# One input block moved between two filter loads, a re-rated planner, rotating PSUM slots, later reloads of q, longer bursts of zero matmuls

## The chip, the cores and the metric

The kernel runs on one core of one Trainium2 chip. The metric is device time in microseconds (us): the kernel before takes 185.58 us, the median of 13 runs that lie between 184.31 and 188.64. Engines are named as in the profile: PE is TensorE (PEld its weight loads), DVE is VectorE, ACT is ScalarE, POOL is GpSimd, SP is SyncE, which here only issues DMAs.

## What is computed

Two branches over the same 2048 x 640 input q are mixed by a gate. Cut to what matters:

```python
# branch A: shift, gate, long convolution by FFT over 2*S points
k_shift = sum(k_pad[:, t:t+S] * shift_k[:, ks-1-t] for t in range(4))
kv = k_shift * v
y  = irfft(rfft(pad(kv)) * rfft(pad(ssm_k)))[:S]   # along the sequence, per channel
a  = q * (y + kv * ssm_D)
# branch B: a token-mixing MLP
h = layernorm(q);  u = gelu(einsum("bsd,sf->bdf", h, w1) + b1)
b = (einsum("bdf,fs->bds", u, w2) + b2).transpose(0, 2, 1)
g = sigmoid((q * gate_w).sum(-1, keepdims=True))
out = g * a + (1 - g) * b                          # 2048 x 640, bf16
```

S is 2048, D (channels) 640, F (hidden tokens) 1536.

## The kernel before, in words

**Work.** The FFT is written as matmuls with a table of sines, `FTB`, followed by adds and subtractions on DVE. In order:

- The filter `ssm_k` is loaded (tile `ssm`), transposed on PE by blocks of 128 channels (`transp`, line 838), evicted from PSUM by ACT into `wT`, and transformed (`fwd` and `fwd_even`, lines 854 and 870) into the spectra `C`, first for half h=0, then for h=1. Each transform group is two or four matmuls of 320 columns and one eviction by ACT ("C<-pp").
- Meanwhile DVE computes the sine arguments (`pint`, line 801 on), which ACT turns into `FTB` (four sines, in the order p = 0, 2, 1, 3), and the layer norm of q: statistics of 16 row tiles ("stats<-X", `ln_tile`, line 913), a reciprocal root on POOL ("rstd"), and the scaling in place ("X<-X,mv,rstd", `ln_apply`, line 932).
- k is loaded (`kn`), permuted by DVE ("kp<-kn", `k_turn`, line 746), transposed by DMA (`KT`), convolved with the four taps on PE ("pp<-KF,KT"), multiplied by v on DVE, and transformed as the filter was.
- The MLP's first layer, 12 output tiles of 32 matmuls each ("pp<-X,ring", called m1 below, line 1057 on), fills PE wherever the above has nothing for it; after it the second layer ("pp<-GT,W", m2, line 1099 on) does so.
- DVE multiplies the spectra (`product`, `cross`, lines 1138 and 1178). Some of the sums are done by accumulating DMAs that POOL issues ("C<-SS", "C<-C"). `invmix` (line 1190) and `inverse` (line 1209) turn the products back; the result is multiplied by q, which is loaded a second time into `q_hi` (rows 0 to 1023) and `q_lo` (the rest), since X has been overwritten by the layer norm. `q_hi` first serves as scratch for the products.

**What orders the work.** No engine chooses at run time. Every operation is entered with an estimated duration and a priority into `_Sched` (line 324), and `run` (line 384) plays the list through: at each moment, each free engine takes the ready operation of lowest priority number. The order found is then emitted, per engine, as the program; each engine (and SP's DMA queue) goes through it strictly in order and waits on semaphores where data are missing. Matmuls of the convolution have their program index as priority, m1 10^6 and more, m2 2x10^6 and more, so the MLP fills gaps. For a DMA the planner takes bytes over a rate (`dma`, line 702: 365 GB/s unless told otherwise), one after another on a single `dma_free` clock, plus 2 us until the data count as landed, and 6 us more for DMAs of POOL (lines 455 to 460). Loads marked `chain=True` keep their program order among one another.

**PSUM.** There are four slots of two banks, `NSLOT = 4`. At most two are held by the MLP and three by the convolution (`limit`, line 333). A slot counts as free when the planner's clock has passed the end of its eviction; the free list is sorted before each take, so the lowest-numbered free slot is used (lines 450 to 453).

**The start.** SP issues `ssm` blocks (0,1), (1,3), (3,5) of half 0 (128, 256 and 256 channels; 256, 512 and 512 KB), then the four blocks of q into `X` (640 KB each), two rows of biases, half 1 of `ssm`, w1, k and so on (lines 765 to 778). Matmuls of zeros (`spin`, line 784) go ahead of each transposition of half 0: (6, 1, 1, 1, 1) of them for the five channel blocks. They have no data to wait for but the zero tile and the PSUM slot.

**The reloads.** The two loads of `q_hi` (line 1261) are entered after the first two products, so each goes out as soon as SP's queue reaches it and its half of the scratch has been read.

Of the kernel before, what the change touches and what calls it, by code (L numbers as in the profile page):

```python
# [18 lines left out]
class _Tracker:  # L19
# [230 lines left out]
        self.dma_sems[name] = sem  # L250
        self.dma_cnt[name] = 0

    def dma(self, stream, out_ap, in_ap, semname, transpose=False, noncontig=False, accum=False):
        reads = [in_ap] + ([out_ap] if accum else [])
        writes = [out_ap]
        acc = self.pre(stream, reads, writes)
        engobj = self.eng[stream]
        sem = self.dma_sems[semname]
        if transpose:
            ins = engobj.dma_start_transpose(out_ap, in_ap)  # L260
        elif accum:
            ins = engobj.dma_start(out_ap, in_ap, accum_op=ALU.add, max_dma_last_dim=2560)  # L262
        elif noncontig:
            with self.nc.allow_non_contiguous_dma(reason="tiny"):
                ins = engobj.dma_start(out_ap, in_ap)
        else:
            ins = engobj.dma_start(out_ap, in_ap)
        ins.then_inc(sem, 16)
        self.dma_cnt[semname] += 16
        v = self.dma_cnt[semname]  # L270
        self.dma_hist[(semname, v)] = dict(self.known[stream])
        src = ("dma", semname, v)
        for reg, mode in acc:
            self.add_record(reg, mode, src)
        return v
# [48 lines left out]
class _Sched:  # L324
# [59 lines left out]
    def run(self):  # L384
# [21 lines left out]
        nfree = list(range(self.NSLOT))  # L406
# [8 lines left out]
        while started < n:  # L415
            while frees and frees[0][0] <= t:
                _, sl, cls = heapq.heappop(frees)
                nfree.append(sl)
                held[cls] -= 1
            nxt = []  # L420
            progress = False
            for e in engs:
                while pend[e] and pend[e][0][0] <= t:
                    _, p, i = heapq.heappop(pend[e])
                    heapq.heappush(ready[e], (p, i))
                if free[e] > t:
                    nxt.append(free[e])
                    continue
                skipped = []
                pick = None  # L430
                while ready[e]:
                    p, i = heapq.heappop(ready[e])
                    op = ops[i]
                    if op.vt is not None and op.vt.slot is None:
                        c = op.vt.cls
                        if not nfree or held.get(c, 0) >= self.limit.get(c, 99):
                            skipped.append((p, i))
                            continue
                    pick = op
                    break  # L440
                for s in skipped:
                    heapq.heappush(ready[e], s)
                if pick is None:
                    if pend[e]:
                        nxt.append(pend[e][0][0])
                    continue
                op = pick
                progress = True
                started += 1
                if op.vt is not None and op.vt.slot is None:  # L450
                    nfree.sort()
                    op.vt.slot = nfree.pop(0)
                    held[op.vt.cls] = held.get(op.vt.cls, 0) + 1
                op.start = t
                if e in ("SP", "QA") or op.lat < 0:
                    issue = 1.2 if e == "POOL" else 0.1
                    s = max(t + issue, dma_free)
                    dma_free = s + op.dur
                    op.end = dma_free + 2.0 + (6.0 if e == "POOL" else 0.0)
                    free[e] = t + issue  # L460
                else:
                    op.end = t + op.dur
                    if op.lock:
                        op.end += max(port["POOL" if e == "DVE" else "DVE"] - t, 0.0)
                        port[e] = op.end
                    free[e] = op.end
                order.append(op)
                if op.vt is not None:
                    op.vt.left -= 1
                    if op.vt.left == 0:  # L470
                        heapq.heappush(frees, (op.end + 0.05, op.vt.slot, op.vt.cls))
                for s in op.asucc:
                    avail[s] = max(avail[s], op.start)
                    s.ndep -= 1
                    if s.ndep == 0:
                        heapq.heappush(pend[s.eng], (avail[s], s.prio, s.idx))
                for s in op.succ:
                    lat = 0.08 if s.eng == e else 0.15
                    if e == "PE" and s.eng == "PE":
                        lat = 0.0  # L480
                    avail[s] = max(avail[s], op.end + lat)
                    s.ndep -= 1
                    if s.ndep == 0:
                        heapq.heappush(pend[s.eng], (avail[s], s.prio, s.idx))
                nxt.append(free[e])
            if not progress:
                c = [x for x in nxt if x > t]
                if frees:
                    c.append(frees[0][0])
                assert c, "schedule stuck: " + str([(o.name, o.eng, o.ndep) for o in ops if not hasattr(o, "end")][:12])  # L490
                t = min(c)
# [19 lines left out]
def _build(nc, A_q, A_k, A_v, A_shift_k, A_ssm_k, A_ssm_D, B_x, B_w1, B_b1, B_w2, B_b2, gate_w, out):  # L511
    Bsz, S, D = A_q.shape
# [9 lines left out]
    with ExitStack() as es:  # L522
# [4 lines left out]
        for i in range(4):  # L527
            h = es.enter_context(nc.psum_tensor(f"pp{i}", [128, 1024], F32))
# [21 lines left out]
        def base_of(h):  # L550
            return T.mem[h.name][1]
# [26 lines left out]
        X = alloc("X", [128, 4, 4, D], BF16)  # L578
# [11 lines left out]
        ssm = alloc("ssm", [128, ND, S], BF16, at=base_of(C[3]))  # L590
# [14 lines left out]
        q_hi = alloc("q_hi", [128, 2, 4, D], BF16, at=base_of(Drow))  # L605
# [96 lines left out]
        def dma(o, i, nbytes, stream="SP", prio=None, sem=None, rate=365.0, chain=False, **kw):  # L702
            if sem is None:
                sem = f"d{ndma[0]}"
                ndma[0] += 1
            if sem not in T.dma_sems:
                T.add_dma_sem(sem, es.enter_context(nc.semaphore(f"s_{sem}")))
            rd = [i] + ([o] if kw.get("accum") else [])
            o_ = SC.add(stream, nbytes / rate / 1000.0, lambda s: T.dma({"QA": "ACT"}.get(stream, stream), o, i, sem, **kw), rd, [o], prio=prio, lat=-1.0, name="dma")
            if chain:  # L710
                if last[0] is not None:
                    o_.after.add(last[0])
                last[0] = o_
            return o_

        def dr(t, off, ap):
            return bass.AP(tensor=t.tensor, offset=t.offset + off, ap=ap)
# [8 lines left out]
            return lambda s: s[:, ci * 512:ci * 512 + 320]  # L726

        def ssm_load(h, a, b):
            dma(ssm[:, a:b, 1024 * h:1024 * h + 1024], dr(A_ssm_k, 128 * S * a + 1024 * h, [[S, 128], [128 * S, b - a], [1, 1024]]), 128 * (b - a) * 2048, chain=True)

        def row8(t, hk):
            return dr(t, (1024 * (hk // 2) + 4 * (hk % 2)) * D, [[8 * D, 128], [1, 4 * D]])
# [2 lines left out]
            return 16 + 128 * (1 - hk % 2)  # L735

        def x_load(hk):
            dma(X[:, hk, :, :], dr(A_q, 512 * hk * D, [[4 * D, 128], [1, 4 * D]]), 128 * 5120, chain=True)

        def w1_load(c, hk):  # L740
            dma(ring[c % 2][:, 4 * hk:4 * hk + 4, :], dr(B_w1, 512 * hk * F + 512 * c, [[4 * F, 128], [F, 4], [1, 512]]), 128 * 4096, chain=True)
# [23 lines left out]
        SSM0 = ((0, 1), (1, 3), (3, 5))  # L765
        SSM1 = ((0, 2), (2, 5))
        small(Drow[:, :], dr(A_ssm_D, 0, [[0, 1], [1, D]]), 1280, "QA")
        small(rows[0:20, 0, 0:128], dr(A_shift_k, 0, [[128, 20], [1, 128]]), 5120, "QA")
        for a, b in SSM0:
            ssm_load(0, a, b)  # L770
        for hk in range(4):
            x_load(hk)
        small(rows[0:4, 1, :], dr(B_b2, 0, [[512, 4], [1, 512]]), 4096, "SP", chain=True)
        small(rows[0:12, 2, 0:128], dr(B_b1, 0, [[128, 12], [1, 128]]), 3072, "SP", chain=True)
        for a, b in SSM1:
            ssm_load(1, a, b)
# [2 lines left out]

        zz = alloc("zz", [128, 512], BF16, at=base_of(GTB))  # L780
        memset("DVE", zz[:, :], 0.0, prio=-1)
        SPIN = (6, 1, 1, 1, 1)

        def spin(k):
            return [((lambda s: s[:, 0:512]), zz[:, 0:128], zz[:, :], True, True)] * k
# [271 lines left out]
        for ft in range(FT):  # L1057
# [20 lines left out]
            if ft in (1, 3, 5, 7):  # L1078
                hk = ft // 2
# [39 lines left out]
        A0 = {0: (C[2], 2), 1: (C[1], 0)}  # L1119
# [10 lines left out]
        def H(hs, c):  # L1130
            h, s = hs
            return V(h, s * SL + 1280 * c, [[SL, 2], [1, 1280]])
# [117 lines left out]
        def chained(f, *a):  # L1250
            n0 = len(SC.ops)
            f(*a)
            new = [o for o in SC.ops[n0:] if o.eng == "DVE"]
            for o in new:
                o.after.update(lastp[-1:])
            lastp.append(new[-1])
# [1 line left out]
        lastp = []  # L1258
        chained(product, A1[1], A1[1], V0[1], tmp_of(q_hi, 0), V1[1])
        chained(product, A1[0], A1[0], V0[0], tmp_of(q_hi, 1), V1[0])  # L1260
        for kt in range(2):
            dma(q_hi[:, kt, :, :], dr(A_q, 512 * kt * D, [[4 * D, 128], [1, 4 * D]]), 128 * 5120)
        acc_dma(A1[1], V1[1])
        acc_dma(A1[0], V1[0])
        chained(product, A0[1], A0[1], V0[1], H(V0[1], 0))
        chained(product, A0[0], A0[0], V0[0])
        for kt in range(2):
            dma(q_lo[:, kt, :, :], dr(A_q, (1024 + 512 * kt) * D, [[4 * D, 128], [1, 4 * D]]), 128 * 5120).after.add(w2last)
# [41 lines left out]
```

## Time and profile before

| what | value |
|---|---|
| median of 13 runs | 185.58 us (184.31 to 188.64) |
| the profiled execution | 184.66 us |
| its span, first to last instruction | 182.7 us |
| around the span (184.66 - 182.7) | 1.96 us |
| granted TensorE clock | 0.997 |
| PE busy / DVE busy / ACT busy / POOL busy | 172.5 / 171.6 / 117.4 / 39.1 us |
| DMA moved | 43.49 MB, mean 238 GB/s |

All moments below are microseconds from the start of the span. A line of the timeline gives start, duration, engine, source line, operation, output<-inputs, shape and count; in brackets stands how long the engine sat idle just before it, and which instruction ended that idle time. Most lines of the kernel record through helpers (L293 is every matmul, L669 every ACT operation, L625 every two-input DVE operation), so tiles tell operations apart, not lines. A busy PE is not PE at its peak: an interval of matmuls contains about 0.17 us of pipeline at its end.

### The profile page before, as it was taken

Reading aid. Unit: us, or ns where it says so; the run is one execution under the profiler, and the core shown is the slowest. Engines: PE = TensorE matmul, PEld = TensorE weight load, DVE = VectorE, ACT = ScalarE, POOL = GpSimd, SP = SyncE. Lnnn points to the kernel's source line nnn. Section 1 sums busy time; section 2 is a strip of 40 time slices with the busy share of each in tenths; the row PEclk is TensorE's granted clock in tenths of the full one; section 3 lists DMA queues with packets and bytes.
Section 4 is the critical chain, followed back from the end, with each engine's and each line's share of the span. In section 5 each row is a group of like instructions: output and inputs, shape, how many; then the busy total and the mean of one; then the engine's idle time right before and its main releaser. Section 6 shows DMA issues by size and latency. Waiting matters only on the chain.

```text
span 182.7 us, 3317 instructions
## 1 busy us (share of the span) xinstructions
PE 172.5 (94%) x1373; PEld 126.3 (69%) x1374; DVE 171.6 (94%) x203; ACT 117.4 (64%) x176; POOL 39.1 (21%) x42
## 2 busy tenths in 40 slices
PE   7878998979999999999999999999999999999991
PEld 2544584576778777776777778888888886778670
DVE  7799895999999999999998999999999979999975
ACT  5799988799989988149999931231312313761660
POOL 4059704000000055000510110403434000054000
PEclk9999999999999999999999999999999999999998
DMA  5999999999999989997499979699999998369584
GB/s 161 367 414 374 389 260 225 289 419 261 170 250 287 166 205 232 240 229 173 115 236 257 272 150 349 147 227 354 201 190 263 229 207 223 129 103 232 95 287 144
DMA packets 38541, 43.49 MB, mean 238 GB/s; under 512 B 15867, under 2 KB 31360, under 8 KB 38528
## 3 DMA queue, kind: packets, MB, share of 16 engines
q1 hardware_dynamic: 33296, 32.16, 59.3%
q0 software_dynamic: 5200, 11.14, 34.4%
q8 instruction: 10, 0.16, 0.4%
q14 instruction: 3, 0.02, 0.0%
q10 hardware_dynamic: 32, 0.01, 0.0%
HBM read 25.87 MB, written 2.62 MB: 156 GB/s over the span
## 4 chain that ended last, share of the span: by engine, by line
PE 38%; DVE 30%; ACT 18%; DMA 9%; issue 3%; DVEq 0%; SPq 0%
PE pp L293 38%; DVE C L625 21%; DMA C<-SS 7%; ACT C L669 5%; ACT gq L669 5%; DVE tm L625 4%; DMA ssm<-in_A_ssm_k_dram 3%; ACT FTB L669 2%; DVE q_hi L625 2%; ACT wT L669 2%; ACT GT L669 2%; DVE gq L625 1%; DVE SS L625 1%; ACT L669 1%; ACT ksh L669 1%
## 5 line engine op out<-in xcount | busy, mean ns | idle before, releaser
L625 DVE TENSOR_TENSOR C<-C 128x2560 bf16<-128x2560 bf16 (+2 forms) x37 | 54.7, 1522 | 1.3 <-DMA C<-SS 1.0
L293 PE MATMUL pp<-X,ring 128*128 128x320 bf16 x384 | 55.3, 299 | 0.0
L293 PE MATMUL pp<-GT,W 128*128 128x320 bf16 x384 | 52.8, 299 | 0.0
L293 PEld LDWEIGHTS pp<-GT,W 128*128 128x128 bf16 x384 | 43.5, 113 | 8.8 <-ACT cgb L669 0.2
L293 PEld LDWEIGHTS pp<-X,ring 128*128 128x128 bf16 x384 | 37.0, 98 | 15.2 <-DVE X L640 0.7
L669 ACT ACTIVATE C<-pp 128x640 bf16<-128x640 f32 x64 | 40.1, 726 | 5.4 <-PE pp L293 5.4
L669 ACT ACTIVATE O<-pp,c,omg 128x640 bf16<-128x640 f32 x15 | 13.3, 886 | 33.8 <-PE pp L293 33.8
L262 POOL DMA_DIRECT2D C<-C x8 | 10.9, 1609 | 46.5 <-DVE C L625 46.0
L293 PE MATMUL pp<-wT,FTB 128*128 128x320 bf16 x112 | 17.8, 300 | 1.6 <-ACT C L669 1.4
L669 ACT ACTIVATE cgb<-pp,gg 128x640 bf16<-128x640 f32 x16 | 12.7, 795 | 8.7 <-PE pp L293 8.7
L293 PEld LDWEIGHTS pp<-wT,FTB 128*128 128x128 bf16 x112 | 9.5, 98 | 8.8 <-ACT C L669 5.2
L919 DVE BATCH_NORM_STATS2 stats<-X 128x6 f32<-128x320 bf16 x32 | 13.7, 464 | 1.5 <-DMA X<-in_A_q_dram 1.5
L669 ACT ACTIVATE GT<-pp,cc 128x640 bf16<-128x640 f32 x12 | 9.4, 787 | 8.3 <-PE pp L293 8.2
L625 DVE TENSOR_TENSOR tm<-C,C 128x2560 bf16<-128x2560 bf16 (+1 forms) x7 | 14.3, 2057 | 0.0
L293 PE MATMUL pp<-C,FTB 128*128 128x320 bf16 x96 | 13.6, 299 | 0.2 <-DVE C L625 0.2
L262 POOL DMA_DIRECT2D C<-q_hi x6 | 5.9, 977 | 31.2 <-DVE C L625 16.2
L293 PEld LDWEIGHTS pp<-C,FTB 128*128 128x128 bf16 x96 | 9.0, 98 | 4.5 <-issue 0.5
L669 ACT ACTIVATE gq<-gq 128x640 bf16<-128x640 bf16 x16 | 11.6, 733 | 0.3 <-DVE gq L625 0.3
L625 DVE TENSOR_TENSOR SS<-C 128x2560 bf16<-128x2560 bf16 x8 | 11.7, 1486 | 0.1
L625 DVE TENSOR_TENSOR C<-tm 128x2560 bf16<-128x2560 bf16 (+1 forms) x9 | 10.6, 1192 | 0.1
L293 PE MATMUL pp<-KF,KT 128*128 128x128 bf16 (+1 forms) x160 | 9.0, 213 | 1.2 <-ACT GT L669 1.1
L669 ACT ACTIVATE wT<-pp 128x1024 bf16<-128x1024 f32 x10 | 9.5, 1034 | 0.8 <-PE pp L293 0.8
(73 smaller groups left out, 185.9 us busy)
## 6 DMA issues: line engine op xcount, KB each, us to landing
ring<-in_B_w_dram SPq DMA_DIRECT2D x12, 512.0 KB, 10.6
W<-in_B_w_dram SPq DMA_DIRECT2D x12, 512.0 KB, 7.3
C<-C POOLq DMA_DIRECT2D x8, 640.0 KB, 11.6
X<-in_A_q_dram SPq DMA_DIRECT2D x4, 640.0 KB, 8.8
kn<-in_A_k_dram SPq DMA_DIRECT2D x4, 640.0 KB, 9.5
out_dram<-O SPq DMA_DIRECT2D x7, 320.0 KB, 2.8
C<-SS POOLq DMA_DIRECT2D x3, 640.0 KB, 12.1
ssm<-in_A_ssm_k_dram SPq DMA_DIRECT2D x3, 512.0 KB, 6.1
```

Source lines behind the costliest of these rows:

```text
L262: ins = engobj.dma_start(out_ap, in_ap, accum_op=ALU.add, max_dma_last_dim=2560)
L293: ins = self.nc.tensor.matmul(ps_ap, lhsT=lhsT, rhs=rhs, start=start, stop=stop, skip_group_check=True)
L625: o_ = SC.add(eng, d, lambda s: T.op(eng, lambda e: e.tensor_tensor(o, a, b, op), rd, [o]), rd, [o], prio=prio, name="tt")
L669: return T.op("ACT", lambda e: e.activation(o, src, func, **kw), rr + [src], ww)
L919: ops.append(SC.add("DVE", 0.38, (lambda o, i: lambda s: T.op("DVE", lambda e: e.bn_stats(o, i), [i], [o]))(o, i), [i], [o]))
```

## The change

Five edits, in one diff:

- block 0 of q is loaded between the second and third filter loads of half 0;
- the planner's rates for some loads are set: 262 GB/s for the first `ssm` load, 195 for the two others of half 0, 385 for half 1, 410 for the blocks of q;
- the free list of PSUM slots is no longer sorted, so slots are taken in the order in which they came free;
- the bursts of zero matmuls are (7, 3, 3, 2, 2) long in place of (6, 1, 1, 1, 1);
- a DMA can be given tiles to wait for (`wait`, treated as extra reads), and the two loads of `q_hi` are entered after the third product and wait for `H(A0[1], 1)`, the half of a product which the accumulating DMA "C<-SS" completes. No arithmetic changes.


```diff
-    def dma(self, stream, out_ap, in_ap, semname, transpose=False, noncontig=False, accum=False):
-        reads = [in_ap] + ([out_ap] if accum else [])
+    def dma(self, stream, out_ap, in_ap, semname, transpose=False, noncontig=False, accum=False, wait=()):
+        reads = [in_ap] + ([out_ap] if accum else []) + list(wait)
...
                 if op.vt is not None and op.vt.slot is None:
-                    nfree.sort()
                     op.vt.slot = nfree.pop(0)
...
-            rd = [i] + ([o] if kw.get("accum") else [])
+            rd = [i] + ([o] if kw.get("accum") else []) + list(kw.get("wait", ()))
...
         def ssm_load(h, a, b):
-            dma(ssm[:, a:b, ...], dr(A_ssm_k, ...), 128 * (b - a) * 2048, chain=True)
+            dma(ssm[:, a:b, ...], dr(A_ssm_k, ...), 128 * (b - a) * 2048, chain=True, rate=(262.0 if a == 0 else 195.0) if h == 0 else 385.0)
...
         def x_load(hk):
-            dma(X[:, hk, :, :], dr(A_q, 512 * hk * D, ...), 128 * 5120, chain=True)
+            dma(X[:, hk, :, :], dr(A_q, 512 * hk * D, ...), 128 * 5120, chain=True, rate=410.0)
...
-        for a, b in SSM0:
+        for a, b in SSM0[:2]:
             ssm_load(0, a, b)
-        for hk in range(4):
+        x_load(0)
+        ssm_load(0, *SSM0[2])
+        for hk in range(1, 4):
             x_load(hk)
...
-        SPIN = (6, 1, 1, 1, 1)
+        SPIN = (7, 3, 3, 2, 2)
...
         chained(product, A1[0], A1[0], V0[0], tmp_of(q_hi, 1), V1[0])
-        for kt in range(2):
-            dma(q_hi[:, kt, :, :], dr(A_q, 512 * kt * D, [[4 * D, 128], [1, 4 * D]]), 128 * 5120)
         acc_dma(A1[1], V1[1])
         acc_dma(A1[0], V1[0])
         chained(product, A0[1], A0[1], V0[1], H(V0[1], 0))
+        for kt in range(2):
+            dma(q_hi[:, kt, :, :], dr(A_q, 512 * kt * D, [[4 * D, 128], [1, 4 * D]]), 128 * 5120, wait=[H(A0[1], 1)])
         chained(product, A0[0], A0[0], V0[0])
```

## Prediction

> **What bounds the kernel now.** I read the busy shares first, then busy time by stretch, then the timeline of the stretches that are not full, then the chain that ended last.
>
> ```profile
> PE 172.5 (94%) x1373; PEld 126.3 (69%) x1374; DVE 171.6 (94%) x203; ACT 117.4 (64%) x176; POOL 39.1 (21%) x42
> PEclk9999999999999999999999999999999999999998
> ```
>
> PE and DVE are equally full over the span. Where they are not full decides. Busy time by stretches of 4 us (PE, PEld, DVE, ACT, POOL, with instruction counts):
>
> ```profile
> 24.00:28.00 4.00, 4.00 (x50) 3.46 (x49) 4.00 (x11) 3.78 (x5) 0.00 (x0) 1.00 1.12 207
> 28.00:32.00 4.00, 3.12 (x21) 1.57 (x19) 1.85 (x8) 3.12 (x5) 2.11 (x3) 1.00 1.19 244
> 36.00:40.00 4.00, 2.77 (x51) 2.35 (x48) 4.00 (x4) 3.99 (x6) 0.00 (x0) 1.00 1.01 415
> 40.00:44.00 4.00, 4.00 (x46) 3.12 (x46) 3.94 (x5) 3.73 (x6) 0.00 (x0) 1.00 0.85 344
> ```
>
> From 40 to 176 PE shows 4.00 in every stretch but one (3.79 in 152:156). So PE's work from there is one block that ends when it ends: only what frees PE before 40 us can move the end, and DVE must keep up. 64 m1 matmuls in a row take 8.86 us, 0.136 us each. Between 22.45 and 38.98 PE does 48 m1 and 16 filter matmuls (8.7 us), 40 transpositions (1.6 and 1.1 us) and 40 tap matmuls (0.95 and 1.35 us): 13.7 of 16.5 us, so about 2.8 us are lost. Before 22.45 ACT sets the pace. The timeline of the start, lines apart:
>
> ```profile
> 8.01 0.29 ACT L669 ACTIVATE cw<-pp 128x140 bf16<-128x140 f32 x1 [1.13 <-PE pp L293]
> 9.42 0.49 DVE L919 BATCH_NORM_STATS2 stats<-X 128x6 f32<-128x320 bf16 x1 [1.52 <-DMA X<-in_A_q_dram]
> ...
> 12.85 3.11 ACT L669 ACTIVATE C<-pp 128x640 bf16<-128x640 f32 x5
> ...
> 24.22 4.69 ACT L669 ACTIVATE wT<-pp 128x1024 bf16<-128x1024 f32 x5 [0.59 <-PE pp L293]
> ...
> 31.68 0.45 DVE L640 TENSOR_SCALAR X<-X,mv,rstd 128x640 bf16<-128x640 bf16 x1 [2.11 <-POOL rstd L625]
> ```
>
> DVE waits 1.52 us for block 0 of q, then is full until 29.6 and scales blocks 2 and 3 from 31.68. ACT is gapless from 8.01 to 23.62. The tail:
>
> ```profile
> 135.42 1.20 POOL L262 DMA_DIRECT2D C<-SS x1 [5.30 <-DVE C L625]
> 147.53 7.10 DVE L625 TENSOR_TENSOR C<-C 128x2560 bf16<-128x2560 bf16 x5 [0.96 <-DMA C<-SS]
> 153.38 4.51 PE L293 MATMUL pp<-C,FTB 128*128 128x320 bf16 x32 [0.21 <-DVE C L625]
> ```
>
> The chain that ended last gives 12.09 us to that C<-SS DMA, but the wait it caused is 0.96 on DVE and then 0.21 on PE; after it PE is full to 178.7.
>
> **The load order.** The DMA view gives issue to landing: filter loads of half 0 land at 0.72+2.9 = 3.6, 1.18+4.7 = 5.9 and about 1.7+6.1 = 7.8; blocks of q at 2.22+7.2 = 9.4, then 10.95, 12.6, 14.2. One block takes about 1.6 us in the row of loads. Exchanged, block 0 lands at 5.9+1.6 = 7.5 and the third filter load at 9.4; everything behind is unchanged in bytes. DVE is free at 7.90, so its whole 1.52 us goes. What is late next: DVE then runs 1.5 us earlier through scaling 0 to 7 (20.05 for 21.55), and meets the permutation of k ("kp<-kn", 23.69 and 25.54). Those loads land at 13.08+10.0 = 23.1 and 13.7+11.0 = 24.7, so slacks were only 0.6 and 0.8. If the order stays, DVE gives 0.9 back there. But the planner's clock for k moves from 21.2 to 22.9 by the new rates (bytes before it over rates, plus 2 us), which puts the permutation behind two more scalings; I take 0.3 back. The second pair of k loads has slack 0.3 (landing 33.25+9.0 = 42.2, use 42.5), so another 0.5 to 1 goes there. DVE's net gain before 45: 0.5 to 1.2; I take 0.7.
>
> PE's gain from it: four m1 weight loads wait for scaled tiles of block 2 at 32.3 to 33.3 (0.17+0.24+0.24 = 0.65 us). With blocks 2 and 3 scaled at about 30.5, that is gone: **-0.65**.
>
> **The third filter load and the new rates.** Transposition of channel blocks 3 and 4 can start at 9.4; before it ran at 8.38 and 9.74, and their evictions ended at 11.96 because ACT was behind. With data at 9.4: PE 0.55, 0.17 drain, eviction 0.94 each: 10.1 to 12.1, 0.1 later at best. In the planner the second load counts as landed at 5.8 (4.3 before) and the third at 10.1 (5.7). So its ACT has a hole from about 8.6 to 10.9, and puts sines there that in this trace ran at 11.81 (1.18 us) and 16.51 (1.16). ACT does the same work in another order. For it: the 1.13 us wait for cw can be filled with the first of these sines, whose arguments are ready at 7.3. Against it: the sine at 11.81 now covers the time between the last wT eviction (11.96) and the first eviction of the transform (12.85); moved ahead, about 0.8 us stands open. Bounds on the end of ACT's stage: -0.7 to +1.3 (both sines ahead, cover gone, bursts exposed). Nearest row is the wait of 1.13 against the cover of 0.8 and the burst below: **0**.
>
> **The bursts.** Seven more zero matmuls. The first six took 2.74 us, 0.43 apart; the next transposition came at 3.85 as they ended, so a seventh costs 0.43 before the first eviction (4.82). Two more for blocks 1 and 2, one each for 3 and 4: three in a row cost 0.82 with drain, so 0.22 each. Block 1's lie in the wait for the load (0.83), those of 3 and 4 in the wait to 9.4, block 2's (0.44) before a transposition that ACT does not need yet. They are part of the estimate of ACT's stage above. The Trainium skill ("TensorE: Matmul & The Clock Gate", part 1) speaks against them: the clock falls to half only after an idle window of some 3.4 us. Here the longest PE wait from 4 to 12 us is 0.83, with the moved load 1.8 at most, and granted clock is 1.00 in each stretch. By the rule the bursts buy nothing; if instead a half clock followed without them, 24 transform matmuls at double 0.136 us would cost 3.3 us more, which no row shows. I take no gain.
>
> **PSUM in turn.** In the transform of half 0, at most three of four slots are held by the planner's clock, and PE waits for an eviction 0.2 us before nearly each group of four; ACT is the pace, so inside the stage nothing changes. At its end PE can be one eviction (0.61 us) further ahead with the fourth slot, begins the transpositions of half 1 that much earlier, and ACT's 0.59 us wait at 24.22 closes: **-0.6**. Bounds: 0 (m1 takes the slot) to -0.6. After 40 us PE waits for no slot longer than 0.2, so nothing there; in the tail the slots are used by evictions of 0.8 us that PE outlasts. The stall of 1.07 at 37.47 comes from a table load (1.28) ahead of a Gelu eviction with all four slots in use: unchanged, 0.
>
> **The reloads.** In SP's queue the first is issued at 122.55, the second at 133.07 and lands 10.6 us later, over the C<-SS DMA (12.1 us; C<-q_hi of the same size took 6.1 and 6.6). Moving the second away takes 640 KB out of that stretch, at 200 to 280 GB/s some 2.5 us. By the row C<-SS could fall to 6.5 us, landing at 142; by the skill ("DMA: Bandwidth & Descriptors", Queues, rings and completion order) a DMA engine alternates between queues but takes each ring in order, so the two C<-C ahead in POOL's queue (landing at 138.8) stay ahead: about 145. Either is before DVE needs it at 146.6, so both give DVE its 0.96, and PE its **-0.2** at 153.38; PE had m2 work for the rest. The new wait holds SP until about 145: behind it stand only q_lo's loads (issued at 150.69) and the stores from 164; the last w2 load (132.59) comes before. Two issues cost about 0.6 us each on SP; landing then takes 5 to 9 us, by 154, with use at 158.75. No cost; if that cover of 4 us went, DVE's multiplication would wait for the excess.
>
> **Sum.** -0.65 -0.6 -0.2 = -1.45. DVE, 0.7 ahead at 45 and 0.96 more at 147.5, carries that. Profiled execution: 184.66 - 1.45 = 183.2. Its own time lies 0.92 below the median 185.58, so the median becomes 184.1.
>
> **Rivals.**
>
> *It fills more (20%).* With q's blocks early and rates that match landings, the plan puts ready matmuls into the holes between 28 and 38: most of the 2.8 us lost, and 0.7 of ACT's start. Then 3 to 4 us: 182.0. For it: waits there come from an order made for other landing times. Against: part of the loss is ACT's (five evictions of 0.64 from 29.78, the table load), which no order of loads removes.
>
> *Nothing arrives (17%).* DVE's 1.5 us are spent waiting for k, whose landings are unmoved, and PE's gain is eaten by a stall of the new order: 185.4.
>
> *Slower (13%).* The third filter load. If both sines go ahead of the last two wT evictions and the bursts delay the first, ACT's transform starts after 13.9 (the old 12.85 plus the one sine that then ran later); each microsecond beyond is one for PE at 22.45, since W of half 0 precedes all m1. At 15.2 (+1.3) it outweighs the gains if PSUM rotation brings nothing and DVE's gain isn't used: 185.6+1.3 = 186.9.
>
> **Numbers.** 50% for the forecast (183.2 to 184.9), the others as given. What this kernel's measurement can tell from no change is about 0.5% (184.65 and 186.5). Faster: most of the 50, all of the 20: 0.63. Same: the rest of the first, the third: 0.24. Slower: 0.13. The range runs from the middle of the second case to just inside the fourth.
>
> **What would show it.** Right: DVE's statistics start at 7.9 without a wait for X; blocks 2 and 3 scaled from about 30.5; ACT's wait at 24.2 gone; m1 from 21.9; DVE without a wait for C<-SS; PE full to the end, everything shifted by 1.4. Wrong: DVE waiting for kn, an eviction of C starting later than 13.9, SP's wait for the reload holding up a w2 load, or a hole in PE after 40.

## Result and profile after

| | before | after |
|---|---|---|
| median | 185.53 us (48 runs, 184.16 to 188.64) | 184.03 us (11 runs, 183.54 to 184.53) |
| profiled execution / its span | 184.66 / 182.7 us | 183.78 / 181.9 us |

The ratio after/before is 0.9928 [0.9903, 0.9952]: 0.7% faster, 1.3 us, against a forecast of 184.1. Ratios leave disturbed executions out, so they differ a little from quotients of medians; for the same reason the profiled execution of one kernel below (ld_fwd) is not read. The forecast's number held; its composition did not. Of its three terms one has the wrong sign, and an item that it does not name cancels that.

The page of after, busy shares, and busy time by stretch (PE, PEld, DVE, ACT, POOL with instruction counts, clock, DMA share, GB/s):

```profile
PE 173.3 (95%) x1380; PEld 128.6 (71%) x1381; DVE 171.3 (94%) x203; ACT 116.9 (64%) x176; POOL 43.7 (24%) x42
```

```profile
28.00:32.00 4.00, 3.32 (x23) 1.61 (x22) 1.85 (x7) 2.69 (x4) 2.11 (x3) 1.00 1.02 212
...
36.00:40.00 4.00, 3.59 (x62) 3.08 (x63) 4.00 (x4) 4.00 (x7) 4.00 (x1) 1.00 1.00 412
...
152.00:156.00 4.00, 4.00 (x31) 3.22 (x30) 3.54 (x3) 2.06 (x3) 0.00 (x0) 1.00 0.88 356
156.00:160.00 4.00, 2.18 (x17) 1.43 (x15) 4.00 (x4) 0.73 (x2) 0.71 (x1) 1.00 0.03 8
```

Two things stand out. PE is fuller at 36 to 40 (3.59 for 2.77), and it has a new hole of 1.8 us at 156 to 160, where it was full before. The timeline of the start, after:

```profile
8.13 0.49 DVE L920 BATCH_NORM_STATS2 stats<-X 128x6 f32<-128x320 bf16 x1 [0.22 <-DMA X<-in_A_q_dram]
...
10.14 1.16 ACT L668 ACTIVATE FTB<-pint,cst 128x1024 bf16<-128x1024 int32 x1
...
13.81 2.49 ACT L668 ACTIVATE C<-pp 128x640 bf16<-128x640 f32 x4 [0.67 <-PE pp L293]
...
22.86 1.30 ACT L668 ACTIVATE C<-pp 128x640 bf16<-128x640 f32 x2 [0.45 <-PE pp L293]
24.04 4.70 ACT L668 ACTIVATE wT<-pp 128x1024 bf16<-128x1024 f32 x5
...
30.39 2.94 DVE L639 TENSOR_SCALAR X<-X,mv,rstd 128x640 bf16<-128x640 bf16 x8 [2.11 <-POOL rstd L624]
```

Block 0 of q arrives 1.3 us earlier, DVE's statistics start at 8.13 with 0.22 of waiting (9.42 and 1.52 before), and DVE keeps that lead: blocks 2 and 3 are scaled from 30.39, not 31.68. All four sines now run before the transform, whose first eviction starts at 13.81 instead of 12.85; but ACT then has no sine left to do between evictions and waits only once, 0.45 us at 22.86, and half 1's evictions start at 24.04 (24.22 before). So at 25 us the whole start is worth 0.18 us. The tail, after:

```profile
134.05 1.20 POOL L262 DMA_DIRECT2D C<-SS  x1 [5.30 <-DVE C L624]
...
143.71 4.29 DVE L624 TENSOR_TENSOR C<-C 128x2560 bf16<-128x2560 bf16 x3
143.97 1.63 SPq L267 DMA_DIRECT2D q_hi<-in_A_q_dram  x2
...
152.17 1.49 DVE L624 TENSOR_TENSOR SS<-C 128x2560 bf16<-128x2560 bf16 x1 [1.37 <-DMA C<-C]
...
153.96 4.29 DVE L624 TENSOR_TENSOR C<-C 128x2560 bf16<-128x2560 bf16 x3 [0.29 <-DMA q_hi<-in_A_q_dram]
...
158.40 2.33 PE L293 MATMUL pp<-C,FTB 128*128 128x320 bf16 x16 [1.82 <-DVE C L624]
```

C<-SS lands at 134.05 + 9.86 = 143.91 (it took 12.09 us before), and DVE no longer waits for it. But DVE's next sums in place ("C<-C" at 153.96) wait for the reload of q_hi, a load whose data they do not use; and PE waits 1.82 us for DVE.

**A ledger.** The first eviction of an m2 tile ("O<-pp") marks one point in every variant: in every trace 488 matmuls end behind it, and the one version in the tables whose PE does not wait there (late_free, below) takes 66.2 us for them. So a span is that moment, plus 66.2, plus what PE loses behind it, plus the closing (PE's last matmul to the end of the span):

| profiled execution | first O | PE lost after it | closing | span |
|---|---|---|---|---|
| before | 111.97 | 0.52 | 4.04 | 182.7 |
| after | 111.04 | 1.97 | 2.71 | 181.9 |
| change | -0.93 | +1.45 | -1.33 | -0.8 |

Each row is one execution. The first column scatters: five executions with the start of the change (last table of the experiments) lie between 110.72 and 111.64, so the lead over this one execution of before is 0.3 to 1.25 us.

The closing is the term that nobody asked for. The end of both kernels, before and after:

```profile
172.54 4.51 PE L293 MATMUL pp<-SS,FTB 128*128 128x320 bf16 x32
...
176.89 1.79 PE L293 MATMUL pp<-GT,W 128*128 128x320 bf16 x12
...
179.60 1.01 DVE L681 SCALAR_TENSOR_TENSOR O<-pp,omg,cgb 128x320 bf16<-128x320 f32 x2
```

```profile
171.44 4.51 PE L293 MATMUL pp<-SS,FTB 128*128 128x320 bf16 x32
...
175.78 3.42 PE L293 MATMUL pp<-GT,W 128*128 128x320 bf16 x24
...
178.57 1.22 DVE L680 SCALAR_TENSOR_TENSOR O<-pp,omg,cgb 128x320 bf16<-128x320 f32 x2
```

Behind the last inverse transform stands a chain of an ACT eviction and DVE multiplications, then the last store. Its DVE end came 1.93 us after PE was through (180.61 against 178.68): PE was not the end. The new plan leaves 24 m2 matmuls for that time in place of 12, so 1.63 us of PE's work moves under the chain, which grows by 0.3.

The last two columns are not independent. The m2 matmuls are a fixed stock: those that stand under the last chain are missing earlier. The plan of after has 296 of them between the first O eviction and the first inverse transform, that of before 304. So a part of what the closing gains is paid for in the holes ahead of it, and the sum of both columns hardly moves: 4.6 before, 4.7 after. What is left of the change in these two executions is the 0.93 of the start.

### The profile page after: what moved, and what is told of

It is laid out like the page before. It is cut to its first block, busy times and chain, and to the rows that moved or that the text cites. A ratio compares the mean times of both kernels' runs of the same rounds, so it can differ in the third digit from the quotient of the medians.

```text
span 181.9 us, 3336 instructions
## 1 busy us (share of the span) xinstructions
PE 173.3 (95%) x1380; PEld 128.6 (71%) x1381; DVE 171.3 (94%) x203; ACT 116.9 (64%) x176; POOL 43.7 (24%) x42
## 4 chain that ended last, share of the span: by engine, by line
DVE 40%; PE 23%; ACT 20%; DMA 11%; issue 4%; POOL 1%; SPq 0%; DVEq 0%
DVE C L624 24%; PE pp L293 23%; DMA C<-SS 5%; ACT C L668 5%; DMA q_hi<-in_A_q_dram 5%; DVE tm L624 5%; ACT gq L668 3%; ACT ksh L668 3%; ACT FTB L668 3%; DVE q_hi L624 3%; ACT wT L668 3%; DVE gq L624 2%; DVE X L639 2%; DVE stats L920 2%; ACT GT L668 1%
## 5 line engine op out<-in xcount | busy, mean ns | idle before, releaser
L293 PE MATMUL pp<-wT,FTB 128*128 128x320 bf16 x112 | 17.2, 299 | 2.0 <-ACT wT L668 1.0
L293 PEld LDWEIGHTS pp<-wT,FTB 128*128 128x128 bf16 x112 | 10.5, 98 | 7.3 <-ACT wT L668 1.4
L262 POOL DMA_DIRECT2D O<-q_hi x4 | 4.8, 1200 | 28.6 <-DVE q_hi L624 28.6
L668 ACT ACTIVATE ksh<-pp 128x1024 bf16<-128x1024 f32 (+1 forms) x12 | 9.8, 894 | 0.6 <-PE pp L293 0.6
```

The source lines that it names most:

```text
L293: ins = self.nc.tensor.matmul(ps_ap, lhsT=lhsT, rhs=rhs, start=start, stop=stop, skip_group_check=True)
L668: return T.op("ACT", lambda e: e.activation(o, src, func, **kw), rr + [src], ww)
```

## Experiments

**Theories on the tail.** A: the reload's `wait` is treated as a read of `H(A0[1],1)`, so whatever overwrites that half must wait until the reload has landed, and the plan is built around it. B (rival): the record is harmless, and the late reload by itself brings the holes, since the inverse needs q_hi.

**late_free**: the reloads wait for C<-SS, but are not recorded as its readers (the same is done in the planner, in the part of the diff that is left out).

```diff
-        reads = [in_ap] + ([out_ap] if accum else []) + list(wait)
+        reads = [in_ap] + ([out_ap] if accum else [])
         writes = [out_ap]
-        acc = self.pre(stream, reads, writes)
+        acc = (self.pre(stream, list(wait), []), self.pre(stream, reads, writes))[1]
...
```

> The change, but the two reloads of q_hi wait for the C<-SS sum without being entered as readers of the product half, so the step that overwrites that half need not wait for them to land. Theory A (the front gained about 1.1 us, and the tail lost 1.6 of what it could have had, because the wait was entered as a read): PE's wait of 1.82 at 158.4 goes, DVE's of 1.37 at 152.2 too; 182.5, that is 1.5 below the change. Theory B (the forecast: front 1.25, tail 0.2, the overwrite costs nothing): 184.0.

Measured: 181.99 us, ratio 0.9826 [0.978, 0.9873], span 180.5. Its timeline and, last line, its chain that ended last (start, length, engine):

```profile
144.30 8.51 DVE L624 TENSOR_TENSOR C<-C 128x2560 bf16<-128x2560 bf16 x6
144.50 1.61 SPq L267 DMA_DIRECT2D q_hi<-in_A_q_dram  x2
...
151.59 4.51 PE L293 MATMUL pp<-C,FTB 128*128 128x320 bf16 x32
```

```profile
41.84 136.03 PE pp L293 x1048
```

The reload goes out as late as in the change (144.50), has landed by 154.05 and is used at 156.96; DVE does its six sums in one run, and PE works from 41.84 to 177.87 without a wait. A holds, B falls: the time is even 0.5 us under A's 182.5. This version beats both kernels, by 1.0% over the change (0.9826/0.9928).

**no_late**: the change with the reloads entered at the old place, without a wait.

```diff
         chained(product, A1[0], A1[0], V0[0], tmp_of(q_hi, 1), V1[0])
+        for kt in range(2):
+            dma(q_hi[:, kt, :, :], ...)
...
-        for kt in range(2):
-            dma(q_hi[:, kt, :, :], ..., wait=[H(A0[1], 1)])
```

> The change with the reloads of q_hi put back where they were before. PE, DVE and ACT then have the very order that they have in late_free; only the reloads' place in SP's queue differs. Theory A: the C<-SS DMA takes about 12 us again and DVE waits about 1 us for it, which PE hides behind second-layer matmuls; 182.6 to 183.2. Theory B: the tail edit is worth 0.2, so 184.2.

Measured: 183.04 us, ratio 0.9893 [0.985, 0.9936], span 181.3. PE, DVE and ACT have the order of late_free, so the pair is clean:

```profile
146.45 7.10 DVE L624 TENSOR_TENSOR C<-C 128x2560 bf16<-128x2560 bf16 x5 [1.02 <-DMA C<-SS]
...
152.29 4.51 PE L293 MATMUL pp<-C,FTB 128*128 128x320 bf16 x32 [0.92 <-DVE C L624]
```

C<-SS takes 12.2 us with the reload beside it and 9.8 without. It lands at 146.43, 1.1 us earlier than before (147.51). But PE comes to the inverse transform 1.8 us earlier, 0.7 by the start and 1.1 by the 8 m2 matmuls that the new plan has fewer ahead of it; so the 0.21 us of before have grown to 0.92. By the ratios the late reload is worth 0.7% (0.9893 to 0.9826), and the recorded read, with the order that is planned around it, costs 1.0% (0.9826 to 0.9928): the edit as made nets a loss of about 0.35%. Of late_free and no_late, run on one chip, all six times of the one lie below all six of the other (181.62 to 182.59, 182.95 to 183.56); the intervals of no_late and after overlap, so the net is less sure than its parts.

**no_fifo**: the change with the free list sorted again; all engine orders are those of the change.

```diff
-                    op.vt.slot = nfree.pop(0)
+                    op.vt.slot = (nfree.sort(), nfree.pop(0))[1]
```

> The change with the free list sorted again. All five engines have the same order as in the change, only the PSUM slots differ. The forecast: 0.6 slower (184.6), ACT's wait ahead of the wT evictions of half 1 back at 0.6. Rival: ACT sets the pace there, nothing is gained: 184.0, within 0.2.

Measured: 185.09 us, ratio 1.0022 [0.9985, 1.0059], span 183.2: the whole gain is gone, more than either expectation had. Where, its timeline shows:

```profile
6.54 0.82 PE L293 MATMUL pp<-zz 128*128 128x512 bf16 x3 [1.12 <-ACT wT L668]
...
22.23 1.25 PE L293 MATMUL pp<-X,ring 128*128 128x320 bf16 x8
```

The zero matmuls ahead of channel block 1 wait 1.12 us for ACT to evict block 0 from the slot that they are given; in the change, with another slot, they run at 4.96. By the planner's clock the second load lands late, so that eviction counts as past and its slot as free, and a sorted list prefers it. m1 starts at 22.23 for 21.03, and the first O eviction at 111.99 for 111.04: 0.95 us, as much as the lead. The span grows by 1.3 us, the ratio by 0.9% (1.7 us); what the profiled execution doesn't show of that stays open.

**no_spin**: the change with the old bursts.

```diff
-        SPIN = (7, 3, 3, 2, 2)
+        SPIN = (6, 1, 1, 1, 1)
```

> The change with bursts of (6, 1, 1, 1, 1) zero matmuls; all orders as in the change. The forecast: no clock is bought, the first eviction starts 0.4 earlier, and ACT, whose chain it heads, ends its filter stage up to 0.4 earlier: 183.6 to 184.0. Rival: PE falls to half clock in the longer wait for the third filter load, 24 matmuls or more at double duration: 185 or more, with a granted clock below 1 before 16 us.

Measured: 183.93 us, ratio 0.9935 [0.9904, 0.9967]. The change once more as a control, **after_again**:

> The change itself, beside the runs below on the same chip: 0.993 of the kernel before, both theories.

Measured: 183.73 us, ratio 0.9927 [0.9892, 0.9962], span 181.7. The bursts buy nothing that can be told. In the profiled execution without them m1 starts at 20.92 (21.03), and the first O eviction at 110.72 (111.04). PE's longest wait up to 20 us is 1.54 there, and the granted clock stays at 1.00 in each stretch of 4 us:

```profile
13.09 2.21 PE L293 MATMUL pp<-wT,FTB 128*128 128x320 bf16 x15 [1.54 <-ACT wT L668]
```

**Theories on the start.** L (the forecast's): the order in which the two loads are issued carries the gain. P: what carries it is the plan, that is, an order of work made for the landing times that the new rates give; the loads' order alone does nothing.

**no_rates**: the change with the planner's old 365 GB/s for all loads.

```diff
-            dma(ssm[...], ..., chain=True, rate=(262.0 if a == 0 else 195.0) if h == 0 else 385.0)
+            dma(ssm[...], ..., chain=True)
...
-            dma(X[...], ..., chain=True, rate=410.0)
+            dma(X[...], ..., chain=True)
```

> The change with the planner's rates of before (365 GB/s for all these loads); everything else as in the change, so the order is planned anew. Theory P: most of the front's gain is lost, 0.997 to 1.003 of before. Theory L: the landing is still early, 0.992 to 0.996.

Measured: 185.77 us, ratio 1.0037 [1.0, 1.0074], span 183.5. Its timeline:

```profile
7.92 0.49 DVE L920 BATCH_NORM_STATS2 stats<-X 128x6 f32<-128x320 bf16 x1 [1.34 <-DMA X<-in_A_q_dram]
...
13.58 2.21 PE L293 MATMUL pp<-wT,FTB 128*128 128x320 bf16 x15 [1.62 <-ACT wT L668]
...
23.12 1.25 PE L293 MATMUL pp<-X,ring 128*128 128x320 bf16 x8
...
159.59 2.33 PE L293 MATMUL pp<-C,FTB 128*128 128x320 bf16 x16 [0.31 <-DVE C L624]
...
177.52 1.79 PE L293 MATMUL pp<-GT,W 128*128 128x320 bf16 x12
```

X lands as early as in the change, but a planner that believes it lands earlier still puts the statistics ahead of work that was ready, and DVE waits 1.34 us all the same. The first O eviction comes at 112.65, and the closing is 4.2 us again, behind 12 matmuls. So both gains of the ledger go with the rates; without them the earlier block, with the other edits in place, is worth nothing that can be told. This run also shows how the ledger's last columns hang together: the reload is recorded as a reader here too, but PE comes later and with 304 m2 matmuls done, as before, so it waits only 0.31 us where the change waits 1.82. Most of the cover for that wait (1.1 us by those 8 matmuls) is what the change has at its end instead.

**ld_back**: the change, planned as it is, with only the two loads exchanged back in the emitted program. **ld_fwd**: the same exchange made in the program of before.

```diff
-        SC.run()
+        SC.run(); ld = [k for k, o in enumerate(SC.order) if o.eng == 'SP'][2:4]
+        SC.order[ld[0]], SC.order[ld[1]] = SC.order[ld[1]], SC.order[ld[0]]
```

> The change with the two loads exchanged back in the emitted order; all engines have the change's order. Theory L: 1.1 lost against the change. Theory P: as much or more, as the plan puts the first m1 matmuls ahead of eight filter matmuls at 21.0, and they now wait for a scaling that is 1.3 later: 1.0 to 1.5 lost against the change. A loss under 0.5 would speak against both.

> The kernel before with nothing changed but the emitted order of two loads: block 0 of q ahead of the third filter load. Every engine has its old order. Theory L (the front's gain is the earlier landing): DVE starts its statistics 1.3 earlier, blocks 2 and 3 are scaled earlier by what the wait for k leaves (0.6 to 1.2), and PE is ahead by 0.6 to 1.1 at 41: 0.994 to 0.997 of before. Theory P (the gain needs the new plan, as PE and ACT still do the filter's transform first): within 0.2% of before, DVE waiting about 0.9 for k.

Measured: ld_back 185.54 us, ratio 1.0034 [0.9994, 1.0074]; ld_fwd 185.99 us, ratio 0.9976 [0.992, 1.0031]. The order alone, in the old program, does nothing that can be told, but its interval holds L's 0.994 to 0.997 as well as P's, so ld_fwd does not decide. Taken out of the new program, the order costs 1.1% (1.0034/0.9927), which is more than either theory had. So no_rates speaks against L, and ld_back shows that the plan without the order brings nothing either: plan and load order have to agree. What ld_back loses is not settled. Its profiled execution, span 182.3, is the fastest of its 12 runs (184.24), and shows only X landing at 8.4, a first m1 at 21.47 and a first O eviction at 111.33, all within the scatter of the same start. In the five longest runs (185.98 to 186.47) the mean granted clock is 0.991; in the other seven it is 1.00, and their median, 184.97, is still 1.2 us over that of after_again. So the lower clock is at most a part of the loss, and why it is lower was not found: none of those runs was profiled.

Not tried: rotation, swap or late reload alone on the old kernel, the change without the swap but planned anew, and late_free with short bursts. So it stays open whether rotation is worth anything under the old plan.

The ledger of the variants (one profiled execution each; with after, the start is the same program in after, after_again, late_free, no_late and, but for the bursts, no_spin, and scatters over 0.9 us):

| | first O | PE lost after it | closing | span |
|---|---|---|---|---|
| after_again | 110.81 | 2.0 | 2.7 | 181.7 |
| late_free | 111.64 | 0.0 | 2.7 | 180.5 |
| no_late | 111.26 | 1.1 | 2.7 | 181.3 |
| no_spin | 110.72 | 1.9 | 2.7 | 181.6 |
| no_fifo | 111.99 | 2.2 | 2.8 | 183.2 |
| no_rates | 112.65 | 0.5 | 4.2 | 183.5 |
| ld_back | 111.33 | 1.9 | 2.8 | 182.3 |

Lost and closing together make 4.6 us in before and 4.6 to 5.0 in every variant that keeps the recorded read, but only 2.7 in late_free and 3.8 in no_late: there, and nowhere else, the tail got shorter.

## Why the prediction was right, and where it was wrong

**Block 0 and the wait for scaled X (-0.65).** The size about held, the place only in part. Block 0 landed at 8.10 (forecast: 7.5), so DVE's 1.52 us wait went to 0.22, not to 0; scaling of blocks 2 and 3 came at 30.39 (forecast: 30.5), no wait for kn appeared, and DVE's lead, forecast as 0.7 at 45 us, was still 1.37 when it issued C<-SS. But the waits for scaled X that I counted (0.17, 0.24, 0.24) are still there in after, 1.3 us earlier; in after_again, where scaling starts at 30.09, they are gone. The weight loads of after, then of after_again:

```profile
31.24 0.11 PEld L293 LDWEIGHTS pp<-X,ring 128*128 128x128 bf16 x2 [0.17 <-DVE X L639]
31.60 0.11 PEld L293 LDWEIGHTS pp<-X,ring 128*128 128x128 bf16 x2 [0.24 <-DVE X L639]
31.95 0.11 PEld L293 LDWEIGHTS pp<-X,ring 128*128 128x128 bf16 x2 [0.24 <-DVE X L639]
```

```profile
30.79 1.05 PEld L293 LDWEIGHTS pp<-X,ring 128*128 128x128 bf16 x8
```

So the forecast's place counts in some executions and not in others. What PE gained in both is that m1 matmuls fit between filter pairs that ACT paces. Before, then after:

```profile
35.45 0.95 PE L293 MATMUL pp<-KF,KT 128*128 128x128 bf16 x16
...
37.47 1.35 PE L293 MATMUL pp<-KF,KT 128*128 128x128 bf16 x24 [1.07 <-ACT GT L669]
...
38.98 2.27 PE L293 MATMUL pp<-KF,KT 128*128 128x128 bf16 x40 [0.15 <-ACT ksh L669]
```

```profile
34.41 1.25 PE L293 MATMUL pp<-X,ring 128*128 128x320 bf16 x8
...
36.17 0.45 PE L293 MATMUL pp<-wT,FTB 128*128 128x320 bf16 x2 [0.51 <-ACT GT L668]
...
36.85 4.33 PE L293 MATMUL pp<-KF,KT 128*128 128x128 bf16 x80 [0.24 <-ACT C L668]
```

The tap matmuls end at nearly the same moment (next PE operation at 41.09 and 41.24), with 56 m1 matmuls done instead of 48, and as many of all others: 8 times 0.136 is 1.09, less 0.15, is 0.94, which is the lead of 0.93 at the first O eviction. The stall of 1.07 that I held for unchanged is shortened in this: the extra m1 group stands where PE stood still for the table load and the Gelu eviction. This is a part of the rival "it fills more", 0.75 us of its 3 to 4 (0.93 less the 0.18 that PE already had at 25 us).

**ACT's filter stage (0).** Right in size: -0.18 at 24, within the bounds. Both sines went ahead and the transform began at 13.81, just under the 13.9 from which the slower rival counts. That mark was not a good one: in after_again it began at 14.07, and the span was no longer (181.7). Eight of the 64 transform matmuls were put behind m1, so m1's start at 21.03 was no gain in itself.

**Bursts (0).** Right. With 7 matmuls fewer (no_spin) PE waited 1.54 us ahead of the transform, and the granted clock of the profiled execution was 1.00 all the same. That agrees with the Trainium skill ("TensorE: Matmul & The Clock Gate", part 1), by which the clock falls after an idle window of some 3.4 us; no PE wait in the lines above is as long. One of the 12 runs of no_spin, its longest (184.45), had a clock of 0.981; it was not profiled.

**PSUM in turn (-0.6).** Needed, but not where I put it. ACT's wait of 0.59 at 24.22 is gone in the change, but not closed: two evictions of C earlier there is one of 0.45 (22.86). In no_fifo the picture is the same (none at 25.25, 0.65 at 24.06), so it was the new plan that moved the wait, and rotation is worth 0.2 us there at most. Rotation pays at 5 us, 0.95 us at the first O eviction, because the new rates make the sorted list choose a slot that is still being evicted. A slot count "by the planner's clock" was the wrong witness: what the rates change is that clock.

**The reloads (-0.2).** This step failed. Its first half was under-sized: C<-SS got 2.2 us shorter, and that is worth about 1 us of PE's time, not 0.2, once PE comes earlier (0.92 of wait in no_late, none in late_free). The landing, 143.91, is near the 145 that I took, but by luck: I had the two C<-C ahead in the queue land at 138.8, while in the trace of before the second lands at 140.73, and DVE's lead put the issue itself 1.37 us earlier, to 134.05. In after that C<-C lands at 138.87 and C<-SS behind it, so the queue's order held. Its second half, "No cost", is wrong in sign. I asked when q_hi is used (158.75) and what is queued behind SP, and named DVE's multiplication as the one to suffer if the cover went. I did not ask what a *read* of `H(A0[1],1)` holds up: the sums of the inverse, which `invmix` (line 1190) writes in place over that half. The planner knows of the new dependence, puts sums of the other half ("SS<-C", 152.17) ahead of the held ones, and these then wait 1.37 us for an accumulating DMA of their own, before the held ones wait 0.29 for q_hi. The front says of `wait` that it is treated as extra reads; each read is also a later write's wait. PE lost 2.0 us behind the first O eviction, 1.45 more than before, and with the record gone 0. The prediction's own sign of being wrong, a hole in PE after 40, came: 1.82 us at 158.40.

**"PE's work from there is one block that ends when it ends"** left out the closing: 4.0 us before and 2.7 after, which no step of mine contains. With the wrong sign in the tail (+1.45 for -0.2) it cancels to within 0.3, in part because it is the same stock of m2 matmuls, moved from the hole to the end.

**From the profile to the median.** I added 0.92, the gap of before. After's profiled execution lies only 0.25 under its median; its runs spread over 1.0 us, those of before over 4.5. Two errors of the sum, span -0.8 for -1.45 and offset 0.25 for 0.92, cancel as well: 183.78 + 0.25 = 184.03. That the median came out within 0.1 us of the forecast is luck. Why the change's runs spread less is open; the bursts are not it (no_spin: 183.44 to 184.45), nor the load order alone (ld_fwd: 183.8 to 187.48). With the slots sorted again the spread is back (no_fifo: 184.76 to 187.43).

## What to carry to other kernels

A dependence entered as a read binds twice: it delays the reader, and it delays every later writer of those bytes until the reader is done. So ask of an added wait who overwrites what it waits for, and if the data are not really read, wait without leaving a record. Where a planner orders the work, a new rate is a new program: look at its far end too, since a planner that moves filler matmuls under the last chain of ACT, DVE and store takes them from the holes ahead of it. Count both together before calling either a gain.

## What the hardware showed unexpectedly

POOL's copy of 128x20 elements took 0.30 us before and 4.91 in the change (times on POOL are rough). Before, then after:

```profile
33.39 0.30 POOL L1028 COPY KT<-KT 128x20 bf16<-128x20 bf16 x1 [1.46 <-DMA KT<-kp]
```

```profile
35.63 4.91 POOL L1029 COPY KT<-KT 128x20 bf16<-128x20 bf16 x1 [4.99 <-DMA KT<-kp]
```

Before, it ran under DVE's scaling, which has one tile as input (and two columns of scalars); so it did in no_rates, in 0.27 us. In the change it lies under DVE operations with two tile inputs, back to back from 33.24, and ends at 40.54, 0.2 us after one of them ("vkv<-ksh,vkv", 40.33) has begun. It took 4.9 to 5.5 us in the six executions with that row of operations, each time ending about 0.2 us into the same one, but 3.06 in no_fifo, where it ended at 38.56, in a gap of DVE (0.26 us ahead of 38.69). That agrees with the Trainium skill ("Advanced Engine Details and Errata", GPSIMD Details), by which POOL shares a read and a write interface with DVE and conflicts with such operations. No run moves the copy alone, so the cause is not shown; it cost nothing visible here.
